# Sharing tiled matmul events: W4's 64-row rests four chunks at a time, W3's rests in one event, the sixth attention group at 120 rows

## The chip, the cores and the metric

One core of one Trainium2 chip. The metric is the device time of the program in microseconds (us); "span" is the time from the first to the last instruction in a profile, some 1.7 us less than the device time. A profile names lines of the kernel's source (L622 is line 622); the changed kernel and each experiment have their own numbering. "Start" always means the start of an instruction in the trace; starts are recorded, while the ends of matmuls are modelled.

## The reference, cut to what matters

```python
S, D, F = 2048, 640, 1728            # rows, width, hidden width of the second MLP
# A: linear attention, 32 heads of 20
kv  = einsum("bhsd,bhse->bhde", phi(k), v);  o = (phi(q) @ kv) / den;  a = o @ wo
# B: mixer MLP
h   = gelu(layernorm(x) @ w1);  x1 = x + shifted(h) @ w2
b   = x1 + gelu(layernorm(x1) @ w3) @ w4
out = g * a + (1 - g) * b            # g: one sigmoid per row
```

All in bf16 with float32 accumulation. The 2048 rows are 16 chunks of 128. What makes the odd sizes: F = 1728 is 13 blocks of 128 and a rest of 64, and D = 640 is five groups of 120 (six heads each) and a sixth of 40.

## The kernel before

Each chunk's output needs W4: 13 full blocks plus the rest of 64 rows, in columns 0 to 512 and 512 to 640. A 64-row rest fills half the array, so two chunks' rests run side by side on the two row halves, and W3's rest (64 columns of weights) runs side by side on the two column halves. Such a run of tiled matmuls, with full-array ones before and after it, is called an event below, row-tiled or column-tiled; a pair of it is two matmuls side by side:

```python
COLS = ((0, 512), (512, D))

def w3_rest(t):                                   # called for t = 0 and t = 2
    ...                                           # block 13 of two row groups, full array
    for dc in range(DC):
        for k in range(2):
            mm(PP[p][FT * k:FT * (k + 1), 0:512], lhsT=w3[:, dc, NF * P:F],
               rhs=lnxT[:, dc, (t + k) * 512:(t + k + 1) * 512], ...,
               tile_position=(0, FT * k))         # column-tiled event
    act(h2x, PP[p][:, 0:512], ACT.Gelu_apprx_tanh)

def w4_units(t, i, last):                         # eight calls, two chunks each
    a_unit(cs[0]); a_unit(cs[1])                  # attention's product for the same chunks
    ps = [alloc(), alloc()]                       # PSUM: four buffers of two banks in all
    for (n0, n1) in COLS:
        for k in range(2):
            mm(PP[p][:, n0:n1], lhsT=h2x[q, cc], rhs=w4[q, NF, n0:n1], start=True, stop=False,
               tile_position=(FT * k, 0))         # row-tiled event
    for k in range(2):
        ...                                       # 13 full blocks, then fin(): VectorE and the output transfer

def kv_unit():
    for g in range(6):
        w = gsz[g]                                # 120 five times, then 40
        for dc in range(DC):
            mm(PP[p][0:w, g * P:g * P + w], lhsT=wv[:, dc, g * GW:g * GW + w], rhs=Gp[...], ...)

def m_unit(g):
    w = gsz[g]
    for (n0, n1) in COLS:
        mm(PP[p][0:w, n0:n1], lhsT=kvT[0:w, g, 0:w], rhs=wo6[0:w, g, n0:n1], start=True, stop=True)
```

## Time and profile before

| | before |
|---|---|
| device time | 266.31 us median of 3 (266.26 to 266.87) |
| span of the profiled run | 265.37 us (that run took 267.08) |
| start of the first W1 matmul | 72.31 us |
| TensorE busy | 259.8 us, 98% |
| row-tiled W4 events, column-tiled W3 events | 8, 2 |

How to read it: TensorE never stops, so the question is only how closely its matmuls follow each other. The prediction below shows the lines.

The timeline of the last 3.5 us of the kernel before (start, length, what):

```profile
261.64 1.08 DVE L606 SCALAR_TENSOR_TENSOR RXH<-pp,omg,RPK 128x512 bf16<-128x512 f32 x2 [1.92 <-PE pp L631]
262.42 0.33 SPq L608 DMA_DIRECT2D out_dram<-RXH  x1
262.75 0.35 ACTq L608 DMA_DIRECT2D out_dram<-RXH  x1
```

VectorE finishes the last chunk in two pieces, 512 columns and 128.

### The profile page before, as it was taken

To read this page: it belongs to the slowest core of one execution; us is meant where nothing else is said; L and a number is where in the kernel's file an instruction comes from. 1 tells how busy PE (TensorE), PEld (TensorE's weight loads), DVE (VectorE), ACT (ScalarE), POOL (GpSimd) and SP (SyncE) were. 2 spreads that over 40 slices of the span, in tenths; PEclk is the share of its full clock that TensorE was granted. 3 is DMA by queue.
4 is the path that set the end of the run, shared out by engine and by line. 5 is a ranking of instruction groups with operands and counts; after the bars stand their busy time and mean duration, and the time that the engine had idled before them with its cause. 6 is when DMAs were issued, how large, how long until landed. Compare 5 with 4: busy or idle time off the path is not lost.

```text
span 265.4 us, 4180 instructions
## 1 busy us (share of the span) xinstructions
PE 259.8 (98%) x1666; PEld 134.8 (51%) x1666; DVE 127.2 (48%) x227; ACT 109.7 (41%) x163; POOL 35.5 (13%) x118
## 2 busy tenths in 40 slices
PE   6999999999999999999999999999999999999995
PEld 2555555555564445554444455555544444555552
DVE  2386659888995257999920044233200002233242
ACT  3466654555454771334977512022034444022020
POOL 7000043030200000446870000000000000000000
PEclk9999999999999999999999999999999999999999
DMA  6899994452252069992542001001000000001001
GB/s 197 162 207 236 367 252 95 99 52 49 50 57 44 11 160 385 340 137 49 108 94 49 0 2 49 25 27 49 27 25 0 0 2 0 25 27 49 25 27 49
DMA packets 42207, 23.95 MB, mean 90 GB/s; under 512 B 31052, under 2 KB 41420, under 8 KB 42188
## 3 DMA queue, kind: packets, MB, share of 16 engines
q1 hardware_dynamic: 41602, 23.16, 36.4%
q10 hardware_dynamic: 586, 0.53, 0.6%
q8 instruction: 13, 0.21, 0.3%
q14 instruction: 6, 0.05, 0.1%
HBM read 12.86 MB, written 3.44 MB: 61 GB/s over the span
## 4 chain that ended last, share of the span: by engine, by line
PE 96%; DMA 2%; DVE 0%; ACTq 0%; ACT 0%; issue 0%
PE pp L637 20%; PE pp L570 20%; PE pp L421 8%; PE pp L596 8%; PE pp L555 8%; PE pp L264 8%; PE pp L255 8%; PE pp L388 8%; DMA RA<-in_A_wqkv_dram 2%; PE pp L579 2%; PE pp L622 1%; PE pp L631 1%; PE pp L586 1%; PE pp L455 1%; PE pp L441 1%; PE pp L468 0%
## 5 line engine op out<-in xcount | busy, mean ns | idle before, releaser
L637 PE MATMUL pp<-RB,RXH 128*128 128x512 bf16 (+1 forms) x390 | 54.4, 299 | 0.0
L570 PE MATMUL pp<-lnxT,RA 128*128 128x512 bf16 x240 | 52.1, 379 | 0.0
L637 PEld LDWEIGHTS <-RXH 128*128 128x128 bf16 x390 | 29.6, 98 | 24.2 <-issue 2.1
L570 PEld LDWEIGHTS <-RA 128*128 128x128 bf16 x240 | 23.4, 98 | 28.1
L599 ACT ACTIVATE RXH<-pp,g_all 128x640 f32<-128x640 f32 x16 | 12.7, 794 | 54.9 <-PE pp L596 54.9
L572 ACT ACTIVATE RXH<-pp 128x1024 bf16<-128x1024 f32 x24 | 24.3, 1020 | 26.7 <-PE pp L570 26.7
L247 ACT ACTIVATE eb<-pp 128x640 bf16<-128x640 f32 (+1 forms) x26 | 21.4, 828 | 25.0 <-PE pp L388 16.1
L264 PE MATMUL pp<-RPK,RXH 128*128 128x512 bf16 (+1 forms) x160 | 25.2, 299 | 0.0
L255 PE MATMUL pp<-RA,RXT 128*128 128x512 bf16 (+1 forms) x160 | 24.1, 299 | 1.0 <-DMA RA<-in_A_wqkv_dram 0.5
L601 DVE SCALAR_TENSOR_TENSOR RPK<-RPK,omg,RXH 128x640 f32<-128x640 f32 x8 | 7.1, 885 | 36.5 <-ACT RXH L599 36.5
L388 PE MATMUL pp<-RXT,RA 128*128 128x512 bf16 x100 | 23.2, 379 | 0.0
L596 PE MATMUL pp<-Mp,pqT 128*128 128x512 bf16 (+1 forms) x160 | 23.1, 299 | 0.0
L555 PE MATMUL pp<-w,RXH 128*128 128x512 bf16 (+1 forms) x160 | 21.9, 299 | 0.0
L601 DVE SCALAR_TENSOR_TENSOR RXT<-RXT,omg,RXH 128x640 f32<-128x640 f32 x8 | 7.1, 885 | 24.6 <-ACT RXH L599 24.6
L421 PE MATMUL pp<-lnxT,RB 128*128 128x512 bf16 x80 | 18.3, 380 | 0.0
L264 PEld LDWEIGHTS <-RXH 128*128 128x128 bf16 x160 | 12.7, 98 | 10.4
L255 PEld LDWEIGHTS <-RXT 128*128 128x128 bf16 x160 | 12.4, 98 | 10.8 <-DVE RXT L322 0.9
L596 PEld LDWEIGHTS <-pqT 128*128 128x128 bf16 x160 | 12.2, 98 | 10.0 <-issue 0.8
L555 PEld LDWEIGHTS <-RXH 128*128 128x128 bf16 x160 | 12.3, 98 | 9.6
L606 DVE SCALAR_TENSOR_TENSOR RXH<-pp,omg,RXT 128x640 bf16<-128x640 f32 x8 | 7.1, 884 | 19.8 <-PE pp L637 19.8
L606 DVE SCALAR_TENSOR_TENSOR RXH<-pp,omg,RPK 128x640 bf16<-128x640 f32 (+2 forms) x9 | 7.3, 810 | 19.1 <-PE pp L637 17.2
L388 PEld LDWEIGHTS <-RA 128*128 128x128 bf16 x100 | 11.1, 117 | 9.1
(107 smaller groups left out, 251.4 us busy)
## 6 DMA issues: line engine op xcount, KB each, us to landing
out_dram<-RXH SPq DMA_DIRECT2D x15, 160.0 KB, 1.8
RA<-in_B_w_dram SPq DMA_DIRECT2D x5, 432.0 KB, 6.7
RA<-in_A_wqkv_dram SPq DMA_DIRECT2D x2, 800.0 KB, 6.8
RB<-in_B_w_dram SPq DMA_DIRECT2D x1, 1120.0 KB
RXH<-in_A_x_dram SPq DMA_DIRECT2D x2, 480.0 KB, 5.1
RB<-in_B_w_dram SPq DMA_DIRECT2D x1, 960.0 KB, 12.2
RB<-in_B_w_dram SPq DMA_DIRECT2D x1, 800.0 KB, 8.5
Mp<-Mscr SPq DMA_DIRECT2D x1, 800.0 KB
```

Of the source, the lines that this page charges most:

```text
L247: act(e[:, 0:n], src, ACT.Exp)
L255: mm(PP[p][:, n0:n1], lhsT=xT[:, dc, c * P:(c + 1) * P], rhs=wkg[:, dc, n0:n1], start=(dc == 0), stop=(dc == DC - 1))
L264: mm(PP[p][:, n0:n1], lhsT=x_sb[:, c, i * P:(i + 1) * P], rhs=pk[:, c, n0:n1], start=(c == 0), stop=(c == NCH - 1))
L388: mm(PP[p][:, tt * 512:(tt + 1) * 512], lhsT=wqp[:, dc, j], rhs=xT[:, dc, t0:t0 + 512], start=(dc == 0), stop=(dc == DC - 1))
L421: mm(PP[p][:, tt * 512:(tt + 1) * 512], lhsT=lh, rhs=lnxT[:, dc, t0:t0 + 512], start=(dc == 0), stop=(dc == DC - 1))
L555: mm(PP[p][:, n0:n1], lhsT=hsT[:, fc, 2 + c * P:2 + (c + 1) * P], rhs=w2[:, fc, n0:n1], start=(fc == 0), stop=(fc == DC - 1))
L570: mm(PP[p][:, k * 512:(k + 1) * 512], lhsT=w3[:, dc, (fc + k) * P:(fc + k + 1) * P], rhs=lnxT[:, dc, t * 512:(t + 1) * 512], start=(dc == ...
L572: act(h2T[:, t % 2, fc:fc + 2, :], PP[p][:].rearrange("p (k s) -> p k s", k=2), ACT.Gelu_apprx_tanh)
L596: mm(PP[p][:, n0:n1], lhsT=pqT[:, j, c * P:(c + 1) * P], rhs=Mp[:, j, n0:n1], start=(j == 0), stop=(j == DC - 1))
L601: nc.vector.scalar_tensor_tensor(x1(c), x1(c), omg[:, c:c + 1], ga, op0=ALU.mult, op1=ALU.add)
L606: nc.vector.scalar_tensor_tensor(oc[:, n0:n1], PP[p][:, n0:n1], omg[:, c:c + 1], x1(c)[:, n0:n1], op0=ALU.mult, op1=ALU.add)
L637: mm(PP[p][:, n0:n1], lhsT=h2T[:, k, fc, cc], rhs=w4[:, fc, n0:n1], start=False, stop=(fc == NF - 1))
```

## The change

The intent is to pay the entry into a tiled mode and the exit from it less often. Four chunks share one row-tiled event. It needs all four PSUM buffers, so it lies in the middle of a group of four chunks; at the start of a group it would wait for them. Both W3 rests share one column-tiled event. The sixth attention group is moved to the last 120 columns of wv and the last 120 rows of wo, with zeros where it overlaps the fifth, so that no matmul with 40 rows or columns of weights is left (in the product with Gp 40 columns are still streamed).

```diff
-    gsz = [GW] * 5 + [D - 5 * GW]
+    G5 = D - GW
+    gof = [g * GW for g in range(5)] + [G5]
+    gw_ = [GW] * 5 + [D - 5 * GW]
...
+    h2x = [RXH[:, 2 * NF * 512:2 * NF * 512 + 512], shs[:, 0:512]]
+    w4z = shs[:, 512:640]
...
-                mm(PP[p][0:w, g * P:g * P + w], lhsT=wv[:, dc, g * GW:g * GW + w], rhs=Gp[:, dc, g * GW:g * GW + w],
+                mm(PP[p][0:GW, g * P:g * P + w], lhsT=wv[:, dc, gof[g]:gof[g] + GW], rhs=Gp[:, dc, g * GW:g * GW + w],
...
-            mm(PP[p][0:w, n0:n1], lhsT=kvT[0:w, g, 0:w], rhs=wo6[0:w, g, n0:n1], start=True, stop=True)
+            mm(PP[p][0:GW, n0:n1], lhsT=kvT[0:GW, g, :], rhs=wo6[0:GW, g, n0:n1], start=True, stop=True)
...
+    nc.gpsimd.memset(w4z[0:FT, :], 0.0)
+    sp.dma_start(w4z[FT:2 * FT, :], B_w4[NF * P:F, 512:D])
...
+    def w3_tail():                       # called once, at t == 0
+        p = alloc()
+        for u in range(2):
+            for dc in range(DC):
+                for k in range(2):
+                    mm(..., tile_position=(0, FT * k), skip_group_check=True)
...
-    def w4_units(t, i, last):            # cut: the old body
+    def w4_group(t, g, ahead, last):
+        ps[0] = alloc()
+        main(0)                          # main(m): chunk m's 13 full blocks
+        a_unit(cs[2])
+        a_unit(cs[3])
+        ps[1] = alloc()
+        main(1)
+        ps[2], ps[3] = alloc(), alloc()
+        for (ms, (n0, n1)) in zip(((0, 1, 2, 3), (2, 1, 0) if last else (2, 3, 0, 1)), COLS):
+            for m in ms:
+                rest(m, n0, n1)          # row-tiled, halves in turn
+        for m in range(2):
+            fin(cs[m], ps[m], 0, D, oc[m])
+            release(ps[m])
+        main(2)
+        ...
+        main(3, COLS[:1])                # the very last chunk only:
+        fin(cs[3], ps[3], 0, 512, oc[3])
+        ps[3] = alloc()
+        mm(PP[ps[3]][:, 512:D], lhsT=hx[:, ...], rhs=w4z, start=True, stop=False)
+        main(3, COLS[1:])
+        fin(cs[3], ps[3], 512, D, oc[3])
```

More of the change, by code (lines that the diff above doesn't have):

```diff
@@ L38 @@
     GW = 120
-    gsz = [GW] * 5 + [D - 5 * GW]
+    NG = 6
+    G5 = D - GW
+    gof = [g * GW for g in range(5)] + [G5]
+    gw_ = [GW] * 5 + [D - 5 * GW]
     NF = F // P
@@ L72 @@
     h2T = RXH[:, 0:2 * NF * 512].rearrange("p (t f s) -> p t f s", t=2, f=NF)
-    h2x = RXH[:, 2 * NF * 512:2 * NF * 512 + 512]
     KP = 648
@@ L193 @@
                                 pattern=[[-1, P]], channel_multiplier=4)
+    nc.gpsimd.memset(kvT[0:GW, 5, gw_[5]:GW], 0.0)
     nc.gpsimd.memset(hsT[:, :, 0:4], 0.0)
@@ L299, in late_loads @@
         sp.dma_start(wo6[0:GW, 0:5, :], A_wo[0:5 * GW, :].rearrange("(g r) d -> r g d", r=GW))
-        sp.dma_start(wo6[0:gsz[5], 5, :], A_wo[5 * GW:D, :])
+        sp.dma_start(wo6[0:GW, 5, :], A_wo[G5:D, :])
         sp.dma_start(w2[:, 0:4, :], B_w2.rearrange("(g c) d -> c g d", c=CG)[0:P])
@@ L437, in kv_unit @@
         p = alloc()
-        for g in range(6):
-            w = gsz[g]
+        for g in range(NG):
+            w = gw_[g]
             for dc in range(DC):
-                mm(PP[p][0:w, g * P:g * P + w], lhsT=wv[:, dc, g * GW:g * GW + w], rhs=Gp[:, dc, g * GW:g * GW + w],
+                mm(PP[p][0:GW, g * P:g * P + w], lhsT=wv[:, dc, gof[g]:gof[g] + GW], rhs=Gp[:, dc, g * GW:g * GW + w],
                    start=(dc == 0), stop=(dc == DC - 1))
@@ L446, in kv_unit @@
         nc.vector.tensor_tensor(kvT[0:GW, 4, :], PP[p][0:GW, 512:512 + GW], bmask[0:GW, :], op=ALU.mult)
-        w = gsz[5]
-        nc.vector.tensor_tensor(kvT[0:w, 5, 0:w], PP[p][0:w, 640:640 + w], bmask[0:w, 0:w], op=ALU.mult)
+        nc.vector.tensor_tensor(kvT[0:GW, 5, 0:w], PP[p][0:GW, 640:640 + w], bmask[0:GW, GW - w:GW], op=ALU.mult)
         release(p)
@@ L452, in m_unit @@
         p = alloc()
-        w = gsz[g]
         for (n0, n1) in COLS:
-            mm(PP[p][0:w, n0:n1], lhsT=kvT[0:w, g, 0:w], rhs=wo6[0:w, g, n0:n1], start=True, stop=True)
+            mm(PP[p][0:GW, n0:n1], lhsT=kvT[0:GW, g, :], rhs=wo6[0:GW, g, n0:n1], start=True, stop=True)
+        w = gw_[g]
         act(Mnat[0:w, g, :], PP[p][0:w, 0:D], ACT.Copy)
@@ L460, in m_move @@
         sp.dma_start(Mscr[0:5 * GW, :].rearrange("(g r) d -> r g d", r=GW), Mnat[0:GW, 0:5, :])
-        sp.dma_start(Mscr[5 * GW:D, :], Mnat[0:gsz[5], 5, :])
+        sp.dma_start(Mscr[5 * GW:D, :], Mnat[0:gw_[5], 5, :])
         sp.dma_start(Mp, Mscr[:, :].rearrange("(q j) d -> q j d", j=DC))
@@ L582, in w3_rest @@
         release(p)
+    def w3_tail():
         p = alloc()
-        for dc in range(DC):
-            for k in range(2):
-                mm(PP[p][FT * k:FT * (k + 1), 0:512], lhsT=w3[:, dc, NF * P:F],
-                   rhs=lnxT[:, dc, (t + k) * 512:(t + k + 1) * 512], start=(dc == 0), stop=(dc == DC - 1),
-                   tile_position=(0, FT * k), skip_group_check=True)
-        act(h2x, PP[p][:, 0:512], ACT.Gelu_apprx_tanh)
+        for u in range(2):
+            for dc in range(DC):
+                for k in range(2):
+                    mm(PP[p][FT * k:FT * (k + 1), u * 512:(u + 1) * 512], lhsT=w3[:, dc, NF * P:F],
+                       rhs=lnxT[:, dc, (2 * u + k) * 512:(2 * u + k + 1) * 512], start=(dc == 0), stop=(dc == DC - 1),
+                       tile_position=(0, FT * k), skip_group_check=True)
+        for u in range(2):
+            act(h2x[u], PP[p][:, u * 512:(u + 1) * 512], ACT.Gelu_apprx_tanh)
         release(p)
@@ L608, in fin @@
         (aq if n0 else sp).dma_start(out2[c * P:(c + 1) * P, n0:n1], oc[:, n0:n1])
-    def w4_units(t, i, last):
-        cs = [4 * t + i, 4 * t + 4 + i]
-        a_unit(cs[0])
-        a_unit(cs[1])
-        ps = [alloc(), alloc()]
-        if last:
-            ps.append(alloc())
-        cc = slice(i * P, (i + 1) * P)
-        for (n0, n1) in COLS:
-            for k in range(2):
-                q = slice(FT * k, FT * (k + 1))
-                p = ps[2] if last and k == 1 and n0 else ps[k]
-                mm(PP[p][:, n0:n1], lhsT=h2x[q, cc], rhs=w4[q, NF, n0:n1], start=True, stop=False,
-                   tile_position=(FT * k, 0))
-        for k in range(2):
-            oc = ocs[ocn[0] % 3]
-            ocn[0] += 1
-            p = ps[k]
-            if last and k == 1:
-                for (p, (n0, n1)) in zip((ps[1], ps[2]), COLS):
-                    for fc in range(NF):
-                        mm(PP[p][:, n0:n1], lhsT=h2T[:, k, fc, cc], rhs=w4[:, fc, n0:n1], start=False,
-                           stop=(fc == NF - 1))
-                    fin(cs[k], p, n0, n1, oc)
-            else:
-                for fc in range(NF):
-                    for (n0, n1) in COLS:
-                        mm(PP[p][:, n0:n1], lhsT=h2T[:, k, fc, cc], rhs=w4[:, fc, n0:n1], start=False,
-                           stop=(fc == NF - 1))
-                fin(cs[k], p, 0, D, oc)
-            release(p)
@@ new lines, in w4_group, with main, rest @@
+    def w4_group(t, g, ahead, last):
+        hx = h2x[t // 2]
+        its = [(i, k) for i in (2 * g, 2 * g + 1) for k in range(2)]
+        cs = [4 * t + 4 * k + i for (i, k) in its]
+        ps = [None] * 4
+        oc = [ocs[(ocn[0] + m) % 3] for m in range(4)]
+        ocn[0] += 4
+        def main(m, parts=COLS):
+            i, k = its[m]
+            for fc in range(NF):
+                for (n0, n1) in parts:
+                    mm(PP[ps[m]][:, n0:n1], lhsT=h2T[:, k, fc, i * P:(i + 1) * P], rhs=w4[:, fc, n0:n1],
+                       start=(m < 2 and fc == 0), stop=(m >= 2 and fc == NF - 1))
+        def rest(m, n0, n1):
+            i, k = its[m]
+            q = slice(FT * k, FT * (k + 1))
+            mm(PP[ps[m]][:, n0:n1], lhsT=hx[q, i * P:(i + 1) * P], rhs=w4[q, NF, n0:n1], start=(m >= 2),
+               stop=(m < 2), tile_position=(FT * k, 0))
+        ps[0] = alloc()
[12 more added lines that the diff above has]
+        main(2)
+        fin(cs[2], ps[2], 0, D, oc[2])
+        release(ps[2])
+        for c in ahead:
+            a_unit(c)
+        if not last:
+            main(3)
+            fin(cs[3], ps[3], 0, D, oc[3])
+            release(ps[3])
+            return
+        main(3, COLS[:1])
+        fin(cs[3], ps[3], 0, 512, oc[3])
+        ps[3] = alloc()
+        mm(PP[ps[3]][:, 512:D], lhsT=hx[:, its[3][0] * P:(its[3][0] + 1) * P], rhs=w4z, start=True, stop=False)
+        main(3, COLS[1:])
+        fin(cs[3], ps[3], 512, D, oc[3])
@@ L650 @@
         w3_rest(t)
+        if t == 0:
+            assert not ln2_d
+            w3_tail()
         while ln2_d:
@@ L654 @@
             scale_q(*sq.pop(0))
-        for i in range(4):
-            w4_units(t, i, t == 2 and i == 3)
+        a_unit(4 * t)
+        a_unit(4 * t + 4)
+        w4_group(t, 0, (4 * t + 2, 4 * t + 6), False)
+        w4_group(t, 1, (), t == 2)
 _INS = ['A_x', 'A_wqkv', 'A_wo', 'B_x', 'B_w1', 'B_w2', 'B_w3', 'B_w4', 'gate_w']
```

## The prediction

> **What bounds the kernel now.** I read the page's busy shares first, then the chain that ended last, then that chain in order of time with the timeline around the odd matmuls.
>
> ```profile
> PE 259.8 (98%) x1666; PEld 134.8 (51%) x1666; DVE 127.2 (48%) x227; ACT 109.7 (41%) x163; POOL 35.5 (13%) x118
> PE 96%; DMA 2%; DVE 0%; ACTq 0%; ACT 0%; issue 0%
> ```
>
> The first line shows TensorE busy 98% of a 265.4 us span, the next engine (VectorE) 48%. The second is the chain of waits by engine: 96% of the span is one unbroken queue of matmuls. The granted clock was 1.000. So nothing but fewer or denser matmuls shortens this kernel, and what another engine gains or loses counts only if it makes TensorE wait. "Busy" does not mean "full speed", though, because a matmul's end is modelled. So I look at how fast matmuls follow each other, in the chain in order of time (start, length, line, count):
>
> ```profile
> 99.76 21.73 PE pp L555 x160
> ...
> 147.39 2.16 PE pp L579 x10
> 149.55 1.20 PE pp L586 x10
> 150.75 2.82 PE pp L596 x20
> ...
> 161.12 2.72 PE pp L596 x20
> 163.84 0.38 PE pp L622 x4
> 164.21 7.17 PE pp L637 x52
> 171.38 2.72 PE pp L596 x20
> ```
>
> The first row is the yardstick: 160 full-array matmuls (80 pairs of one 512-column and one 128-column) in 21.73 us are 0.2716 us a pair; single starts in the trace are 216 ns after a 512 and 56 ns after a 128. One W4 unit, from 161.12 to 171.38, takes 10.26 us. It holds 10 + 26 full pairs and one row-tiled event (L622: four 64-row matmuls, two beside two, so one pair's worth). At the yardstick that is 37 x 0.2716 = 10.05. The other 0.21 us is the event's overhead. The timeline shows where it lies:
>
> ```profile
> 163.76 0.11 PEld L622 LDWEIGHTS <-RXH 64*128 64x128 bf16 x4 [0.26 <-issue]
> 163.77 0.45 PE L622 MATMUL pp<-RB,RXH 64*128 64x512 bf16 x4
> 164.14 0.39 PEld L637 LDWEIGHTS <-RXH 128*128 128x128 bf16 x4 [0.26 <-issue]
> ```
>
> Elsewhere weights load under the running matmul; on both sides of the event the weight loader sits idle 0.26 us for nothing but "issue". From the starts: the first tiled matmul comes 152 ns after the last full 128-column one (56 is normal: +96). The first full matmul comes 149 ns after the last tiled one (+93), and about 23 ns go as first-gap delays (226 and 223 instead of 216; 226 again for the first full one, less rounding and the 3 ns between tiles). Sum 0.21 us, in each of 8 events. The column-tiled event (L586, W3's rest) has the same shape:
>
> ```profile
> 149.48 0.79 PEld L586 LDWEIGHTS <-RA 128*64 128x64 bf16 x10 [0.42 <-issue]
> 150.68 0.39 PEld L596 LDWEIGHTS <-pqT 128*128 128x128 bf16 x4 [0.41 <-issue]
> ```
>
> In starts: +93 on entry, 1203 ns for five side-by-side pairs of 512 that need 5 x 216 = 1080 (so +123, exit included), and +10 on the first full matmul after it: 0.225 us, twice in the kernel.
>
> The small matmuls of attention show the same at 40 rows or columns:
>
> ```profile
> 84.52 0.55 PE pp L455 x4
> 89.93 0.65 PE pp L455 x4
> 90.58 4.42 PE pp L421 x20
> ```
>
> L455 x4 with all 120-row weights takes 0.55; with the sixth group (40 x 40) as its second half it takes 0.65 here, and the L421 block behind it carries the exit: 20 x 0.216 = 4.32, not 4.42. In starts: 745 ns against 545, plus 6.
>
> **What the Trainium skill says.** "TensorEngine Tiling (Array Packing)", Key Properties: "Changing tiling mode (not just tile) drains the TensorE". The trace agrees: about 95 ns at each entry and exit, whether rows or columns are tiled. "TensorE: Matmul & The Clock Gate", Part 3, says that matmuls on different tiles run concurrently, some 4 ns apart; here L622's two start 3 to 4 ns apart, and the second pair follows 226 ns after the first. The same page's Back-to-back issue gap gives N/2.4 + 2.5 ns for a warm matmul, 216 and 56; the trace has just these. Its section on Fast Weight Load wants 128 weight columns; loads of 120 columns take up to 145 ns here (L441) against 98, yet follow each other every 55 ns, so 120-wide groups cost no more than that.
>
> **The change part by part.** The order of instructions differs only where the diff says so, and the number of matmuls is the same but for their forms.
>
> (1) W4's rests: 8 events become 4. Each new one holds four chunks: eight matmuls as four side-by-side pairs (two of 512, two of 128), 2 x 272 = 544 ns of streaming, the same work as two old events. It has one entry and one exit. Saved: 4 x 0.212 = 0.85 us. It sits between two full W4 runs instead of between the attention product and W4, but the entry follows a full 128-column matmul as before.
>
> (2) W3's rests: two column-tiled events of five pairs become one of ten, at the first. The second pass goes straight from full to full. Saved: 0.225 us.
>
> (3) Sixth kv group. In the product with Gp, the last five of the 30 matmuls (40 columns of weights) start 148, 42, 25, 25, 25 ns apart and the next line follows after 113: 378 ns. With 120 weight columns and 40 moving ones there is no mode change; I take the 55 ns of their 25 neighbours, limited by the weight load: 55 x 6 = 330. Saved 48, plus 6 on the next first gap: 0.05 us. If the shorter stream counted, it would be up to 0.13.
>
> (4) Sixth product with wo: 745 becomes 545, plus 6 ns: 0.21 us.
>
> (5) Added: the very last 128-column rest cannot be in the event (its PSUM buffer is not yet free), so it runs as a full 128-row matmul against zero-padded weights. One 56 ns matmul lies in the last 128-column run, while its event keeps two 128-steps (pair, then a single): no saving there. Is it hidden? The final VectorE step starts at 262.367 in the trace, 257 ns after the last matmul's start at 262.110; a VectorE step released by a matmul starts 257 ns after it elsewhere too (258.579 to 258.836). So the end hangs on TensorE: -0.056 us.
>
> (6) Added off the path: 100 KB more of wo, 16 KB of W4 rows, two small GpSimd memsets, a wider mask product. TensorE does not wait for these.
>
> Sum: 0.85 + 0.225 + 0.05 + 0.21 - 0.06 = 1.28 us. 266.31 - 1.28 = **265.03 us**, a gain of 0.5%.
>
> **Rivals.** (A) The longer row-tiled event is not as dense as I assume: the before never has more than two pairs in one event, both with weights loaded on entry, so the third and fourth may each wait for a weight load (92 to 96 ns in this mode). That would be up to about 100 ns x 2 x 4 = 0.8 us lost and 265.8. Against it: the column-tiled event keeps a pitch of 216 ns through five pairs after a first gap of 240, and its weight loads lie under the stream; in full mode 128-column pairs follow each other every 56 ns. Only the 128-column steps are at risk, perhaps 40 ns per event; 0.16 us as a likely worst case.
>
> (B) PSUM waits. All four double-bank buffers are held through an event. The third and fourth come from two attention products, which ScalarE empties in 794 ns each, and a W4 run of 13 pairs (3.5 us) lies in between. The next products use buffers whose VectorE steps (885 ns) begin after the event, under another 3.5 us run. Slack over 1 us everywhere; I expect no wait. If each group did wait half a microsecond, the time would be 267.
>
> (C) W3's merged rest comes too early. It now reads all 16 transposed chunks at about 149 us. The last transpose is issued at 139.6 and lands in 2.6 us by the median of before: 7 us of slack. But the new W4 load shifts which earlier load each later transfer must follow in the queue, so the first four transposes could go out a little later; the fourth is issued at 116.0 and its reader starts at 121.3, 2.7 us of slack after landing. A shift under 1 us vanishes there; if it were 3 us, the gain would fall to 1.
>
> (D) The drain is not per event but per switch of a chunk's tile, then (1) saves nothing: 265.9. Inside today's event the tile alternates at 3 ns, which speaks against it.
>
> **Range and chances.** The sizes are measured starts, repeated within 4 ns over eight and two events, so the sum should hold to 0.2 us unless A or C bites. The run-to-run spread is the larger part: three runs of before lie between 266.26 and 266.87. I put 264.7 to 265.5, with more room above than below since the rivals all cost time. 2% would be 5.3 us; no part reaches that. Faster by over 2%: 0.01; within 2%: 0.98; slower: 0.01.
>
> **What would show it.** Four row-tiled events instead of eight, each with first-to-next-full about 650 ns (544 + 106) and the same 0.26 us idle of the weight loader on both sides: step 1. One column-tiled event of about 2.28 us: step 2. L441's 30 matmuls in about 1.675 us from first start to next line instead of 1.723: step 3. All three pairs of the wo products at 0.55: step 4. The last 128-column run one matmul longer: step 5. I would be wrong if row-tiled events last 0.75 us or more (A), if TensorE shows idle time with ScalarE, VectorE or a DMA as releaser between 121 and 262 us (B, C), or if the weight loader's idle spells around W3's and W4's tiled events do not fall from ten events to five.

## The result, and the profile after

The changed kernel took 265.11 us (median of 6, 264.81 to 265.71) against 266.36 us for the kernel before on the same chip (median of 6, 266.26 to 266.87). The ratio is 0.9953, with a 95% interval of 0.9937 to 0.9969; it is the mean time of one kernel's fast runs over the mean of the other's of the same rounds, so not quite the ratio of the medians. The predicted time was 265.03.

The page of the changed kernel: busy time, then the chain of waits by engine.

```profile
PE 256.4 (97%) x1634; PEld 135.9 (52%) x1666; DVE 126.9 (48%) x227; ACT 109.6 (42%) x163; POOL 36.1 (14%) x120
PE 97%; issue 1%; ACT 0%; DVE 0%
```

TensorE is still the bound. Its count went from 1666 to 1634 although the program has as many matmuls as before and the weight loads are all 1666 there: 32 matmul records, about one in 52, are missing from this trace. Most of them look like 0.05 us of "issue" in the chain, which makes up most of the 1%, and no time was lost there: the next start comes where a present record would have put it, and the second profile of this kernel has all 1666 records and the same stretch from the first W1 matmul on (table below). The chain in order of time:

```profile
89.03 0.55 PE pp L458 x4
89.57 4.32 PE pp L426 x20
...
148.43 2.28 PE pp L595 x20
150.71 2.82 PE pp L606 x20
...
163.31 0.65 PE pp L638 x8
163.96 3.64 PE pp L632 x26
```

The third pair of wo products (L458) takes 0.55 like the others, and the W1 block after it 4.32 instead of 4.42. The one column-tiled event (L595) takes 2.28 us. The row-tiled event (L638) holds eight matmuls in 0.65 us, 544 ns of streaming and some 0.1 us of overhead, the rest of which shows as neighbours that are 0.1 us too long (3.64 for 13 pairs). The timeline shows the weight loader idle before a row-tiled event as it was before, 0.26 us. At the exit it now sits idle only from 163.79 to 163.89, 0.10 us, because the last weights of the event are loaded later; this view does not mark so short a gap. Around the column-tiled event both pauses are there as before:

```profile
163.24 0.55 PEld L638 LDWEIGHTS <-RXH 64*128 64x128 bf16 x8 [0.26 <-issue]
163.25 0.72 PE L638 MATMUL pp<-RB,RXH 64*128 64x512 bf16 x8
...
163.89 0.11 PEld L632 LDWEIGHTS <-RXH 128*128 128x128 bf16 x2
```

```profile
148.36 1.87 PEld L595 LDWEIGHTS <-RA 128*64 128x64 bf16 x20 [0.42 <-issue]
150.64 0.11 PEld L606 LDWEIGHTS <-pqT 128*128 128x128 bf16 x2 [0.41 <-issue]
```

In starts: the first tiled matmul 151 ns after the last full one (56 + 95), the first full one 649 ns after the first tiled one (544 + 105), and 227 instead of 216 ns to the one after that: 211 ns for an event of four chunks, as much as the 212 for two.

**Spans mislead here.** The two profiled spans differ by 2.3 us (265.4 and 263.1), far more than the times do. The stretch before the first W1 matmul differs by 0.8 us of that, and it differs as much between runs of one kernel. In some runs TensorE waits there for the first weights; the timelines of two runs of the kernel before, and of an experiment whose start the change cannot have slowed, read:

```profile
6.69 0.70 PE L255 MATMUL pp<-RA,RXT 128*128 128x512 bf16 x4 [0.55 <-DMA RA<-in_A_wqkv_dram]
```

```profile
6.86 0.70 PE L255 MATMUL pp<-RA,RXT 128*128 128x512 bf16 x4 [0.93 <-DMA RA<-in_A_wqkv_dram]
```

```profile
7.20 0.70 PE L260 MATMUL pp<-RA,RXT 128*128 128x512 bf16 x4 [0.96 <-DMA RA<-in_A_wqkv_dram]
```

In the profile of the changed kernel there is no such wait at all; in its second profile the first two 512-column matmuls of that stage are followed after 427 and 426 ns, as in the warm-up, and 216 ns is reached later. The first W1 matmul starts anywhere from 71.2 to 72.8 us in the fourteen profiles, in no order that follows the kernels. From there on each kernel repeats within 0.01 us, and all the readings below use that stretch. It is cut at the start of the last 512-column matmul:

| run | first W1 matmul starts at | from there to the last 512-column matmul | from that to the end | both |
|---|---|---|---|---|
| before | 72.31 | 188.916 | 4.146 | 193.062 |
| before, second profile | 72.48 | 188.913 | 4.148 | 193.061 |
| changed | 71.49 | 187.545 | 4.059 | 191.604 |
| changed, second profile | 72.15 | 187.544 | 4.054 | 191.598 |

So the change is worth 1.371 us on TensorE's path and 0.087 us at the end, 1.46 us in all. The lowest times come near that: 264.81 us in both sets of rounds of the changed kernel, 266.26 and 266.14 in those of before (1.45 and 1.33 us apart). The medians (1.25 and 1.20 us apart in the two sets) carry the scatter of the start.

### The profile page after: what moved, and what is told of

Read it like the earlier page. It is cut to its first block, busy times and chain, and to the rows that moved or that the text cites. A ratio compares the mean times of both kernels' runs of the same rounds, so it can differ in the third digit from the quotient of the medians.

```text
span 263.1 us, 4153 instructions
## 1 busy us (share of the span) xinstructions
PE 256.4 (97%) x1634; PEld 135.9 (52%) x1666; DVE 126.9 (48%) x227; ACT 109.6 (42%) x163; POOL 36.1 (14%) x120
## 4 chain that ended last, share of the span: by engine, by line
PE 97%; issue 1%; ACT 0%; DVE 0%
PE pp L632 21%; PE pp L576 20%; PE pp L260 8%; PE pp L606 8%; PE pp L269 8%; PE pp L426 8%; PE pp L561 8%; PE pp L393 8%; PE pp L585 2%; PE pp L316 1%; PE pp L638 1%; PE pp L595 1%; PE pp L446 1%; PE pp L458 1%; PE pp L326 0%
## 5 line engine op out<-in xcount | busy, mean ns | idle before, releaser
L632 PE MATMUL pp<-RB,RXH 128*128 128x128 bf16 (+1 forms) x407 | 57.7, 297 | 0.7 <-issue 0.3
L632 PEld LDWEIGHTS <-RXH 128*128 128x128 bf16 x416 | 31.8, 98 | 24.5
L260 PE MATMUL pp<-RA,RXT 128*128 128x130 bf16 (+1 forms) x156 | 23.5, 297 | 0.7 <-ACT RXT L328 0.5
L606 PE MATMUL pp<-Mp,pqT 128*128 128x128 bf16 (+1 forms) x158 | 22.9, 298 | 0.1
L561 PE MATMUL pp<-w,RXH 128*128 128x128 bf16 (+1 forms) x157 | 21.7, 297 | 0.2
L269 PEld LDWEIGHTS <-RXH 128*128 128x128 bf16 x160 | 12.7, 98 | 10.4
L561 PEld LDWEIGHTS <-RXH 128*128 128x128 bf16 x160 | 12.3, 98 | 9.5
L255 DVE TENSOR_SCALAR eb<-eb 128x640 bf16<-128x640 bf16 (+1 forms) x26 | 9.5, 364 | 11.4 <-ACT eb L252 11.4
L256 DVE SCALAR_TENSOR_TENSOR RPK<-pp,eb 128x640 bf16<-128x640 f32 x16 | 13.2, 825 | 2.1
```

Of the source, the lines that this page charges most:

```text
L256: nc.vector.scalar_tensor_tensor(dst, src, 0.0, e[:, 0:n], op0=ALU.max, op1=ALU.add)
L260: mm(PP[p][:, n0:n1], lhsT=xT[:, dc, c * P:(c + 1) * P], rhs=wkg[:, dc, n0:n1], start=(dc == 0), stop=(dc == DC - 1))
L269: mm(PP[p][:, n0:n1], lhsT=x_sb[:, c, i * P:(i + 1) * P], rhs=pk[:, c, n0:n1], start=(c == 0), stop=(c == NCH - 1))
L561: mm(PP[p][:, n0:n1], lhsT=hsT[:, fc, 2 + c * P:2 + (c + 1) * P], rhs=w2[:, fc, n0:n1], start=(fc == 0), stop=(fc == DC - 1))
L606: mm(PP[p][:, n0:n1], lhsT=pqT[:, j, c * P:(c + 1) * P], rhs=Mp[:, j, n0:n1], start=(j == 0), stop=(j == DC - 1))
L632: mm(PP[ps[m]][:, n0:n1], lhsT=h2T[:, k, fc, i * P:(i + 1) * P], rhs=w4[:, fc, n0:n1], start=(m < 2 and fc == 0), stop=(m >= 2 and fc == N ...
```

## The experiments

Theory 1: every change of TensorE's tiling mode, into it or out of it, costs some 95 ns, and nothing else matters. Rivals: the gain comes from the new place and order of W4's rests; a wait for PSUM or for a transfer eats part of it; the start makes the measured difference. All kernels gave correct results. All in one table, with what the trace says first, because the timing cannot resolve a tenth of a per cent. One run each of kv_only (270.34 us) and split8 (269.96 us) counts as slow and is left out of the ratios.

| run | to the last 512 | from that to the end | both, against changed | ratio of times to before (95%) |
|---|---|---|---|---|
| kv_only | 188.619 | 4.150 | +1.165 | 0.9982 (0.9964 to 1.000) |
| w3_only | 188.686 | 4.147 | +1.229 | 1.0001 (0.9978 to 1.0024) |
| w4_only | 188.064 | 4.062 | +0.522 | 0.9970 (0.9949 to 0.9991) |
| split8 | 188.392 | 4.082 | +0.870 | 0.9965 (0.9945 to 0.9986) |
| pad_full | 188.815 | 4.144 | +1.355 | 0.9982 (0.9943 to 1.002) |
| at_start | 190.361 | 4.074 | +2.831 | 1.0047 (0.9994 to 1.0101) |
| no_z | 187.548 | 5.049 | +0.993 | 0.9974 (0.9932 to 1.0017) |
| adj | 188.188 | 4.067 | +0.651 | one run, 266.21 us |
| spare | 187.547 | 4.160 | +0.103 | 0.9967 (0.9931 to 1.0004) |
| after_again | 187.544 | 4.054 | -0.006 | 0.9963 (0.9931 to 0.9996) |
| before_again | 188.913 | 4.148 | +1.457 | one run, 267.26 us |
| lanes | 187.543 | 3.931 | -0.130 | 0.9928 (0.9907 to 0.9949) |

**Each part alone: kv_only, w3_only, w4_only.** The edit is the diff above, one part at a time on the kernel before.

```diff
 kv_only:  + kv_unit, m_unit, gof/gw_, the zeros in kvT, the 120-row load of wo; W3 and W4 as before
 w3_only:  + w3_tail at t == 0, two h2x buffers; the rest as before
 w4_only:  + w4_group, w4z;  W3's rest still once for t = 0 and once for t = 2, kv as before
```

> Only the sixth attention group at 120 rows; W3's and W4's rests as before. Theory 1 (each change into or out of a tiled mode costs TensorE some 95 ns, nothing else matters): TensorE's path shorter by 0.05 to 0.09 us in the product with Gp and by 0.21 us in the products with wo, so 0.26 to 0.30 us in all, ratio to before about 0.9989 to 0.9990. Rival, that the 100 KB of extra wo or the wider mask product cost something: a wait of TensorE between 70 and 100 us appears, and the gain is below 0.2 us.

> Only W3's two rests in one column-tiled event; all else as before. Theory 1: one column-tiled event of about 2.28 us from its first matmul to the next full one, none at the second pass, 0.225 us less, ratio 0.9992 (below what timing resolves, so the trace decides). Rival, that the earlier read of all chunks waits for a transpose: an idle spell of TensorE with a DMA or ScalarE as its releaser just before the event, and no gain.

> Only W4's rests in four events of four chunks (with the zero-padded last piece); W3 and attention as before. Theory 1: 4 x 0.212 - 0.056 = 0.79 us less than before, ratio 0.9970. With the two other single changes the gains add up to 1.3 us. Rival (start-up decides the measured gain): the ratio differs from this by more than 0.001 and the trace shows the difference before the first W1 matmul.

Measured on the stretch to the last 512-column matmul: 188.916 - 188.619 = 0.297, 188.916 - 188.686 = 0.230 and 188.916 - 188.064 = 0.852 us. They add up to 1.379; the change has 1.371. So the parts do not disturb each other, and none brought a wait with it. To the last matmul, with the padded one in it, w4_only gained 0.795 (expected 0.79). The times bear out w4_only and leave the two small parts open, as expected (w3_only's interval spans 1). In kv_only the chain shows both of its pieces:

```profile
77.10 1.67 PE pp L445 x30
78.76 2.17 PE pp L425 x10
```

In the kernel before, the W1 block behind the 30 matmuls took 2.26 with the exit in it; the 30 themselves show no gain in this view, because their exit was booked to that block and their last five were short. In starts the stretch from the 25th matmul to the next line fell from 378 to 305 ns: the first of the five now comes 55 ns after the 25th, the second 30 ns after that, the rest 55 ns apart. I had assumed 55 for all.

**split8: the number of events or their place.**

```diff
+        # rests of chunks 0 and 1 after main(1), rests of chunks 2 and 3 after main(2): eight events, all mid-group
-        for (ms, (n0, n1)) in zip(((0, 1, 2, 3), ...), COLS):
-            for m in ms:
-                rest(m, n0, n1)
```

> The changed kernel with each four-chunk event split again in two events of two chunks, both inside the group between full W4 runs, so the order of chunks, the buffers and the place stay those of the change and only the number of mode changes goes back to eight events. Theory 1: 0.85 us slower than the changed kernel, 0.47 us faster than before, ratio to before 0.9982. Rival (the place between W4 runs and the new order bring W4's gain, not the number of events): as fast as the changed kernel, ratio 0.9953.

The path grew by 188.392 - 187.545 = 0.847 us. The chain shows two events of the old length around one full run, and each neighbour lengthened by 0.1:

```profile
164.64 0.38 PE pp L638 x4
165.02 3.64 PE pp L632 x26
168.66 0.38 PE pp L638 x4
169.03 2.82 PE pp L606 x20
```

So it is the number of events; the place and the order bring nothing. The ratio of times (0.9965) lies below the expected 0.9982, with an interval that holds both, and the rival's 0.9953 too; the trace decides.

**pad_full: no tiling at all.**

```diff
-            mm(..., lhsT=hx[q, i * P:(i + 1) * P], rhs=w4[q, NF, n0:n1], ..., tile_position=(FT * k, 0))
+            mm(..., lhsT=hx[:, i * P:(i + 1) * P], rhs=w4p[k][:, n0:n1], ...)     # other 64 rows are zeros
```

> The changed kernel without any row tiling: each chunk's 64-row rest runs as full 128-row matmuls against weights padded with zeros, same places, same buffers. Theory 1: no mode change is left in W4, the weight loader has no idle spell there, and each group pays four pairs of 272 ns instead of two pairs and 212 ns: 3 x 0.33 + 0.28 = 1.27 us slower than the changed kernel, so about level with before (ratio 0.9998). Rival (the events' overhead is not the mode change but something of the place, such as the wait for PSUM or the load of new weights): an overhead around the rests stays, and it is slower than before.

The path grew by 188.815 - 187.545 = 1.270 us, to three figures the expected sum. The weight loads of the rests now run without a pause on either side:

```profile
163.20 1.13 PEld L638 LDWEIGHTS <-RXH 128*128 128x128 bf16 x8
...
164.29 0.15 PEld L633 LDWEIGHTS <-RXH 128*128 128x128 bf16 x2
```

So the overhead is the mode change and nothing of the place. It also says when tiling pays: an event costs 0.21 us and saves 136 ns per chunk, so from two chunks on.

**at_start: the event where the old one was.**

```diff
-        ps[0] = alloc()
-        main(0)
         a_unit(cs[2])
         a_unit(cs[3])
-        ps[1] = alloc()
-        main(1)
-        ps[2], ps[3] = alloc(), alloc()
+        ps[0], ps[1], ps[2], ps[3] = alloc(), alloc(), alloc(), alloc()
         ...                              # rests, then main(0), main(1), main(2), main(3)
```

> The changed kernel with the four-chunk event at the start of each group, right after the attention products, instead of in its middle. The number of events is the same four. If only the number of mode changes counted, it would be as fast as the changed kernel (ratio 0.9953). What I expect: the event then needs all four buffers at once, and the last is emptied by ScalarE (794 ns, begun some 257 ns after the last matmul's start): a wait of about 0.7 us in each of four events, 2.8 us slower than the changed kernel, ratio to before about 1.006, with ScalarE as the releaser of TensorE inside the event.

Measured 190.361 - 187.545 = 2.816 us, 0.70 per event. The timeline of the first event names the releaser:

```profile
156.03 0.60 PE L638 MATMUL pp<-RB,RXH 64*128 64x512 bf16 x3
...
156.98 0.48 PE L638 MATMUL pp<-RB,RXH 64*128 64x512 bf16 x5 [0.35 <-ACT RXH L609]
```

The fourth matmul, the other half of the second pair, starts 725 ns after the third (3 ns in the changed kernel). The view puts 0.35 us of it to ScalarE, which empties the buffer of the last attention product; the modelled end of the third hides the rest. So rival B of the prediction is a real cost, and placing the event mid-group is what avoids it: same events, 2.8 us apart.

**no_z: is the zero-padded piece needed?**

```diff
-        ps[3] = alloc()
-        mm(PP[ps[3]][:, 512:D], lhsT=hx[:, ...], rhs=w4z, start=True, stop=False)
         main(3, COLS[1:])               # same buffer as the 512 columns; its rest is in the event
```

> The changed kernel without the zero-padded last piece: the last chunk's 128-column rest stays in its event and in the same buffer as its 512 columns. One matmul of 56 ns less on TensorE, but the last 128-column run then waits for VectorE to read the 512 columns of that buffer (begun 0.42 us after the last 512 start, 0.75 us long): about 1.0 us of wait, 0.9 us slower than the changed kernel, ratio to before about 0.9987. If buffers were told apart by bank and no wait arose: 0.06 us faster than the changed kernel.

The last 128-column run starts 1.22 us after the last 512 start, released by VectorE, and the end comes 0.99 us later:

```profile
260.78 0.75 DVE L613 SCALAR_TENSOR_TENSOR RXH<-pp,omg,RPK 128x512 bf16<-128x512 f32 x1 [1.92 <-PE pp L629]
...
261.58 0.89 PE L629 MATMUL pp<-RB,RXH 128*128 128x128 bf16 x13 [0.84 <-DVE RXH L613]
```

The wait is one that the program asks for: its semaphores guard the buffer of two banks as a whole. This version also has no load of w4z, and by that one check more at the end, some 0.07 of the 0.99 us (see spare and lanes). So the 56 ns of padding buys some 0.9 us.

**adj: from one tiling to the other without full matmuls between.**

```diff
+        if t == 0 and g == 1:
+            w3_tail(1)                   # W3's second rest, column-tiled, straight before the row-tiled event
         ps[2], ps[3] = alloc(), alloc()
```

> The changed kernel with W3's second rest as a column-tiled event of its own, straight before a row-tiled event of W4. One look at the starts: from the last column-tiled 512 to the first full matmul it is 312 ns (216 + 96), and a row-tiled event starts 96 ns late after a full matmul. If going from column to row tiling costs one drain, the first row-tiled matmul starts about 312 ns after the last column-tiled one; if leaving and entering are paid apart, about 408 ns. The event will then also wait about 0.5 us for ScalarE to empty the buffer of the column event.

```profile
183.21 0.79 PEld L594 LDWEIGHTS <-RA 128*64 128x64 bf16 x10 [0.26 <-issue]
...
184.41 0.12 PEld L636 LDWEIGHTS <-RXH 64*128 64x128 bf16 x4 [0.41 <-issue]
...
185.17 0.48 PE L636 MATMUL pp<-RB,RXH 64*128 64x512 bf16 x5 [0.15 <-ACT shs L597]
```

The first row-tiled matmul starts 311 ns after the last column-tiled one, which is 216 + 95: the price of one mode change, not of two. The event then waits for ScalarE to empty the column event's buffer (531 ns in place of 3 between the two halves of its second pair), so this order as it stands is slower. I found no order that keeps the one change and avoids that wait, with four buffers.

**spare: an attempt to do without the padded matmul and without the wait.**

```diff
+            dst = PP[ps[1]][:, D:D + P] if last and m == 3 and n0 else PP[ps[m]][:, n0:n1]
...
-        for ... (2, 1, 0) if last
+        for ... (2, 1, 0, 3) if last
-        mm(PP[ps[3]][:, 512:D], ..., rhs=w4z, start=True, stop=False)
```

> An attempt to beat the changed kernel: the last chunk's 128-column rest goes back into its row-tiled event, as the partner of the odd third one, into 128 columns of another chunk's PSUM buffer that nothing uses. No zero-padded matmul, no extra load, and VectorE's read of the last 512 columns is in another buffer, so no wait. Theory: 56 ns less than the changed kernel from the first W1 matmul to the last matmul (188.43 us), the end moves with it; timing cannot resolve it (ratio to before about 0.995). Rival (the last 128-column run waits for VectorE all the same): about 0.9 us slower than the changed kernel.

The last matmul starts 0.886 us after the last 512-column one, where the changed kernel has 0.942: the 56 ns are gone from TensorE, and there is no wait. Yet the end comes 4.160 us after that 512-column matmul and not 4.059, 0.10 us later. So the end does not hang on the last matmul. Two things follow from the table. First, pad_full has the padded matmul as well (0.941) and ends at 4.144, as the kernel before does at 0.885 and 4.146: 56 ns more or less in the last run do not reach the end. Second, there are two groups of ends: 4.14 to 4.16 for the kernel before, kv_only, w3_only, pad_full and spare, and 4.05 to 4.08 for the changed kernel, w4_only, split8, at_start and adj. What goes with this split is the number of queued transfers: the traces hold 93 issues in each kernel of the first group and 94 in each of the second, by the load of w4z. (The expectation of lanes below counts 86, 87 and 89; the traces have 93, 94 and 96. The differences are the same.)

**after_again, before_again: what repeats.** Both kernels unaltered.

> The changed kernel unaltered, to see what repeats. Theory (all of the gain lies after the first W1 matmul; the scatter of the times is in the loads at the start): 188.49 us within 0.02 from the first W1 matmul to the last matmul, as in its first profile, while the time to the first W1 matmul moves by some tenths of a microsecond. If the change altered the start, that stretch would be shorter again by 0.8 us than in the kernel before.

> The kernel before unaltered, one look: 189.80 us within 0.02 from the first W1 matmul to the last matmul, the first W1 matmul anywhere between 71.2 and 72.8 us as in the other runs.

After the first W1 matmul both repeat within 0.01 us (table above; to the last matmul 188.486 and 189.799 us, as expected), and the start moved from 71.49 to 72.15 in the changed kernel and from 72.31 to 72.48 in the one before. So the start is scatter, not part of the change.

**lanes: the end.** Queued transfers signal on eight semaphores in turn, and at the end SyncE checks these one after the other.

```diff
+        if c in (0, 4):                  # two early chunks: send 512 and 128 columns apart
+            sp.dma_start(out2[c * P:(c + 1) * P, 0:512], oc[:, 0:512])
+            sp.dma_start(out2[c * P:(c + 1) * P, 512:D], oc[:, 512:D])
+            return
```

> The changed kernel with the output transfers of two early chunks split in two each (512 and 128 columns), so that the program has 89 queued transfers instead of 87 and the last two take the last two of the eight completion semaphores that the SyncE checks in turn at the end. Theory (the 87 against 86 transfers, not the matmuls, made the stretch from the last 512-column matmul to the end 0.09 us shorter in the changed kernel: 4.06 against 4.15 us, one check fewer after the last landing): two more checks go before it, some 65 ns each, so 3.93 us, and 0.13 us less than the changed kernel after the first W1 matmul (191.47 instead of 191.60). Rival (the 0.09 us comes from something else, such as the later last piece): 4.06 us stays. Timing alone cannot resolve it.

Measured 3.931 us and 191.474 us, as expected. The end of the changed kernel in the timeline, and SyncE's checks in the views of the final line, first for the kernel before, then for the changed one, then for this one (count, durations in ns, first and last start in us):

```profile
259.25 0.22 PE L667 MATMUL pp<-shs 128*128 128x128 bf16 x1
...
260.23 0.33 SPq L618 DMA_DIRECT2D out_dram<-RXH  x1
260.61 0.35 ACTq L618 DMA_DIRECT2D out_dram<-RXH  x1
```

```profile
L682 SPq EVENT_SEMAPHORE  x7: 17/28/28, 264.2 to 265.3; - x7
```

```profile
L716 SPq EVENT_SEMAPHORE  x7: 17/28/28, 260.6 to 263.0; - x7
```

```profile
L720 SPq EVENT_SEMAPHORE  x7: 17/28/28, 261.1 to 263.4; - x7
```

In the kernel before, the first check is recorded at 264.2, after the 512-column transfer that was issued at 262.42 has landed, and all others follow it. In the changed kernel one check passes at 260.6, straight after the issue at 260.23, so one fewer is left for the end; in this experiment three pass there (261.09, 261.16, 261.22). Each check takes about 65 ns (264.34, 264.41, 264.48 in the kernel before).

The traces' record of landings shows the rest. From the landing of the second transfer to the end it takes 1.03 to 1.05 us with four checks still to begin (before, kv_only, w3_only, pad_full, spare), 0.965 to 0.977 with three (changed, w4_only, split8, at_start, adj) and 0.85 with one (lanes). In all of these the second transfer lands 0.17 to 0.18 us after the first, whether it is issued 1.53 us after the last 512-column matmul or, behind the padded one, 1.58; that is where the 56 ns go. The end therefore hangs on the landing of the last transfers and on how many checks are queued behind it. This version took 264.94 us (median of 6, lowest 264.51) against 266.54 for the kernel before on the same chip. It was not timed beside the changed kernel; that it is the faster of the two, by 0.13 us, is read from the traces.

## Why the prediction was right, and where not

The predicted 265.03 us met 265.11, and every term on TensorE's path but one had its size. But the sum was 1.28 us where the traces hold 1.46: 0.04 more in step 3, the 0.056 of step 5 that never reached the end, and 0.087 at the end that was not forecast. The scatter of the start hid this difference in the medians, so that the two figures meet within 0.08 us is in part luck.

- **Step 1, W4's events, 0.85 us: right.** w4_only gives 0.852, and split8 gives 0.847 back. Event length 649 ns against the stated 650.
- **Step 2, W3's rests, 0.225 us: right.** w3_only gives 0.230; the event takes 2.28 us as stated.
- **Step 3, the product with Gp, 0.05 us: mis-sized.** Steps 3 and 4 together gave 0.297 in kv_only; the wo products have 0.209 of it, so this one has 0.09. The term that failed is "55 x 6 = 330": one of those distances is 30 or 31 ns, so the 30 matmuls take 1.650 us and not 1.675, and the full matmul behind them is followed after 215 ns rather than 220. Most of the distances did stay at 55 ns with 40 moving columns and 120 weight columns, where 40 weight columns had allowed 25; that the weight load sets them fits this, but was not tested apart. The "0.13 if the shorter stream counted" was not the way it went.
- **Step 4, the wo products, 0.21 us: right** (545 for 745 ns in starts, and 4414 for 4423 in the block behind).
- **Step 5, -0.06 us: right on TensorE, wrong at the end.** The statement "So the end hangs on TensorE" failed: VectorE's last step does, but the end hangs on the last landings and the checks after them. spare and pad_full show that the 56 ns are hidden: the end comes 4.160 us after the last 512-column start without them and 4.144 with them.
- **Step 6 said that the extra transfers cost nothing off the path. The count of them mattered**: one more transfer shifted the last two by one semaphore, and one check fewer is left after the last landing. That is some 0.07 of the 0.087 us at the end; the rest is no more than the scatter of the first landing, 2.90 to 2.95 us after the last 512-column start in all profiles. I had not thought of it; lanes settles it.
- **Rival A** (the longer event is less dense) fell: the second pair of 512 follows after 226 ns, as the second pair did before, the pairs of 128 after 216 and 56, and no pair waits for weights. One sign of step 1 did not come: "the same 0.26 us idle of the weight loader on both sides" holds on entry only (0.10 us on exit), though the exit still costs 95 ns in starts. **Rival B** (PSUM) is real at another place, 0.70 us an event in at_start, and absent in the change. **Rival C** fell: no idle time before the merged W3 event. **Rival D** (the drain per chunk) fell with step 1.
- **The range** was meant to cover mostly run-to-run spread, and that was its use: single runs of the changed kernel lie from 264.81 to 265.71 in the first set and up to 267.75 in the second.

The Trainium skill's sentence on the drain ("TensorEngine Tiling (Array Packing)", Key Properties) carried the argument: it is the change of mode that counts, and not the change of tile. The runs agree with it: 3 to 4 ns from tile to tile inside an event, some 95 ns at its ends, none left in pad_full, one paid in adj. What happens inside the 95 ns stays open. The first weight load of the new form is recorded only 1 to 5 ns before its first matmul (163.763 and 163.767 us in the kernel before), so no run here tells an array that empties from a weight load that cannot go ahead.

## What to carry to other kernels

Where TensorE is the bound, look for pauses of the weight loader with no releaser: in both kernels, after the first W1 matmul, each one over 0.2 us marks a change of tiling mode, about 95 ns, though not every change shows one, so that the starts decide; and it pays to gather tiled matmuls until PSUM is full and to put that event where the buffers have long been emptied. Operands that are merely narrow can cause such a change without a tile position in the source; widening them with zeros was cheaper. Two such events are left in both kernels and were not touched, one of 32 weight columns (L468 of the kernel before: entered 310 ns after a 512-column start and left after 312, where 216 is the stream) and one of 32 rows (L482: 312 and 317). When the differences are below half a per cent, compare the stretch of the trace after a common early instruction, not spans or medians, and look at what follows the last matmul before counting on it.

## What the Trainium skill lacked or had wrong

- "TensorEngine Tiling (Array Packing)" says that a change of mode drains TensorE, without a size: the runs show 93 to 96 ns on entry and on exit, with rows or columns tiled, 0.21 to 0.23 us for an event with its first gaps, and one such change (311 ns where 216 is the stream) straight from column to row tiling.
- The same page speaks of tiling as something configured. The 40 x 40 matmuls of the kernel before had no tile position and paid the same (146 ns in place of 55 to enter, 149 for 56 to leave); at 120 rows and columns they paid nothing.
- "TensorE: Matmul & The Clock Gate", Back-to-back issue gap, gives 81 ns (N = 128) and 131 ns (N = 512) for a sustained stream of weight loads and matmuls. Every stream of full matmuls here has 55 to 56 and 215 to 216, which is its formula for the isolated gap.
- The same page's LDWEIGHTS section gives a duration by columns (P/1.2, so 100 ns for 120 columns by that formula). The trace has 132 to 145 ns for 120 columns outside the fast load; in a stream they follow each other every 55 ns, also where only 40 columns are streamed (25 ns with 40 weight columns), and no page that I read states it.
- No page that I read has the checks at the end of a program: about 65 ns for each completion semaphore checked after the last landing, so that the number of queued transfers, 93, 94 or 96, moved the end from 4.15 to 4.06 and 3.93 us after the last 512-column matmul.
